# Where the token numbers of a routed mixture-of-experts kernel are multiplied in

## The chip, the core and the metric

The kernel runs on one core of a Trainium2 chip. The metric is the device time of one execution, in microseconds. It is compared as the median of several executions of the same program.

## The reference

Three layers follow each other: a chunked attention, a soft mixture of experts, and a top-2 routed mixture of experts. The change touches the third alone, which is given here without its first lines (three matrix products and a log1p that yield `noisy_logits`, 3072 x 8):

```python
N, D, E, F = 3072, 512, 8, 1024
top2 = np.argpartition(-noisy_logits, 2, axis=1)[:, :2]
top2_l = np.take_along_axis(noisy_logits, top2, axis=1)
top2_l = top2_l - top2_l.max(-1, keepdims=True)
top2_w = np.exp(top2_l)
top2_w /= top2_w.sum(-1, keepdims=True) + 1e-09
out = np.zeros((N, D), dtype=np.float32)
for e in range(E):
    for k in range(2):
        mask = top2[:, k] == e
        if not mask.any():
            continue
        h = np.maximum(x[mask] @ w1[e], 0.0)
        out[mask] += top2_w[mask, k, None] * (h @ w2[e])
```

So each of 3072 tokens has two experts, and 6144 token-expert pairs go through a 512-1024-512 network of their expert.

## The kernel before, in words

`experts` sorts the 6144 pairs into 48 tiles of 128 slots, with experts in an order of ranks 0 to 7 that depends on the data. Rank 0 fills the first six tiles by construction, ranks 1 to 7 the rest. A few more tiles stand behind a branch and are not used with this input. Instructions are issued in the order of the source, so each engine runs its own instructions in the order in which `experts` calls the helpers.

**A tile in the loop** (index `n`, tile `i`): `gather(i)` fetches 128 rows of a table by token number (POOL, an indirect DMA through `idx`). `ct(i)` transposes them on PE, with a copy on ACT. `l1(i)` is eight matmuls with the rank's first matrix `G`, then a relu into `hi` on ACT, and `lo(i)` puts the rest that float16 loses into `lo` on DVE. `l2(i)` is 24 matmuls: eight of `hi` with the float16 second matrix, eight of `hi` with that matrix's low part, and eight of `lo` with the float16 second matrix. `yv(i)` scales on ACT, and `put(i)` adds the rows into two output tensors by two indirect DMAs on POOL. In the loop, step `n` issues gather(n+6), ct(n+2), l1(n+1) and l2(n), in this order on PE: ct, l1, l2. Tiles 0 to 5 use `G` in place; from tile 6 on `gcopy` (SP) copies the rank's `G` into the buffer `C` or `CT`, and the first layer of tile 6 waits for that.

**Preparing a rank's weights** (`prep_*`, rank `rk`): a product of all slot outputs with the first matrix (`prep_g`, PE), maxima of both matrices (`prep_gmax`, `prep_max`, DVE; `bound`, ACT), two transposes on PE that spread the maxima over the partitions (`prep_row`, `prep_all`) with a reduction on DVE between them, scale factors (`prep_s`, `prep_inv`), the scaled `G` (`prep_gs`, ACT and DVE), and the second matrix in four parts, each as a float16 high part (`prep_hi`, ACT) and a low part (`prep_lo`, DVE, L428). `plan(n, ...)` puts such a step into loop step `n` ahead of `l2`; `mid(n, ...)` puts it inside `l2`, ahead of its last eight matmuls.

**Finding the token of each slot.** `bases` and `positions` (DVE) give each pair its slot, split into a column `ns` within a tile and a tile number `tq`. `spread_s` makes 48 one-hot matrices of 128 x 128 from `ns` (L544 on DVE, L537 and L540 on ACT), `tiles` (L812) compares `tq` with the tile numbers, and POOL multiplies the result by the token numbers `K["val"]` (L813). `inverse` sums 48 products of the two on PE (L647), and `finish_idx` (DVE, L655 to L658) turns that into `idx` for tiles 6 and up, which the gathers of tiles 6 and later need. `tile_tables` (L780 to L797) gives each tile its rank (`rti`). `wide_w` (POOL) makes the gate weights that go into the table. All of this stands between the first tiles of rank 0, which have an index of their own.

Of the kernel before, what the change touches and what calls it, by code (L numbers as in the profile page):

```python
# [14 lines left out]
OP = mybir.AluOpType  # L15
# [10 lines left out]
NT = N // 128  # L26
# [9 lines left out]
NSL = NTL + 2  # L36
# [2 lines left out]

RB = 12  # L40
NA0, NP0 = 7, 5
NA2, NP2 = 16, 0
ORDER = [('qk', 29), ('mx', 29), ('s0', 29), ('tr', 31), ('sub', 29), ('exp', 29), ('s1', 29), ('av', 27), ('nrm', 27), ('lt', 5), ('ltc', 5), ('qk', 30), ('max', 0), ('at', 28), ('atc', 28), ('mx', 30), ('qk', 31), ('col', 0), ('at', 29), ('s0', 30), ('sub', 30), ('atc', 29), ('pc', 15), ('exp', 30), ('colc', 0), ('av', 28), ('bc', 0), ('nrm', 28), ('pc', 14), ('xt', 26), ('dsub', 0), ('mx', 31), ('xtc', 26), ('s1', 30), ('ex', 0), ('sub', 31), ('ldv', 31), ('exp', 31), ('at', 30), ('s0', 31), ('atc', 30), ('av', 29), ('xt', 28), ('xt', 27), ('mm', 0, 0, 0), ('nrm', 29), ('s1', 31), ('at', 31), ('atc', 31), ('xtc', 27), ('xtc', 28), ('av', 30), ('nrm', 30), ('xt', 29), ('av', 31), ('xt', 30), ('mm', 0, 0, 1), ('xtc', 29), ('xtc', 30), ('lg', 6), ('nrm', 31), ('mm', 0, 1, 1), ('xt', 31), ('lgc', 6), ('xtc', 31), ('es', 0), ('lg', 7), ('lt', 6), ('lgc', 7), ('lt', 7), ('ltc', 6), ('esp', 0), ('mm', 0, 2, 1), ('ltc', 7), ('mm', 0, 3, 1), ('mm', 0, 1, 0), ('max', 1), ('col', 1), ('mm', 0, 2, 0), ('colc', 1), ('bc', 1), ('dsub', 1), ('fac',), ('mm', 0, 3, 0), ('ex', 1), ('mm', 1, 0, 0), ('facx',), ('out', 0, 0), ('out', 0, 1), ('es', 1), ('mm', 1, 1, 0), ('esp', 1), ('out', 1, 0), ('w',), ('mm', 1, 0, 1), ('mm', 1, 1, 1), ('sit', 0), ('out', 1, 1), ('sitc', 0), ('sit', 1), ('sitc', 1)]
CF = {}
C16 = {}
# [261 lines left out]
def experts(tc, nc, C, CT, SOT, sog, wgn, nz, zt, table, mw1, mw2, out, K, K16, rw, rt, ew, ps):  # L307
# [119 lines left out]
        w2, hi, lo = w2p(rk, part)  # L427
        stt(lo, w2, sc[:, rk, 5:6], hi, op0=OP.mult, op1=OP.subtract)  # L428

    def prep_lop(rk, part):  # L430
        w2, hi, lo = w2p(rk, part)
        t = W2r[:, 7 * 4096 + 3072:8 * 4096]
        nc.gpsimd.tensor_tensor(t, w2, bc(sc[:, rk, 5:6], 1024), OP.mult)
        nc.gpsimd.tensor_tensor(lo, t, hi, OP.subtract)

    s4 = T(5)

    def bound(x, vec=False, half=None):
# [365 lines left out]
        vt(t, s4[:, 2:4], AX.X, OP.max)  # L804
        tt(sc[:, rk, 1:2], sc[:, rk, 1:2], t, OP.max)

    J2 = cut(48, NA2, NP2)
    o2 = oh_t[:, :, T0:NSL]

    def tiles(k):  # L810
        o, q = [x[:, NT * k:NT * k + NT] for x in (o2, tq)]
        tt(o, bc(K16["t128"][:, None, T0:NSL], NT, NSL - T0), bc(q[:, :, None], NT, NSL - T0), OP.is_equal)  # L812
        nc.gpsimd.tensor_tensor(o, o, bc(K["val"][:, :, None], NT, NSL - T0), OP.mult)  # L813

    finish_idx(0, T0)
    gather(0)
# [13 lines left out]
        gather(i)  # L830
    ct(0)
    prep_hi(0, 2)
    bases()
    ns, tq = positions()
    gcopy(0)
    gcopy(1)
    gcopy(2)
# [5 lines left out]
    gates2()  # L843
    prep_inv(0)
    ts(gw0, gw0, sc[:, 0, 6:7], 2.0 ** -10, op0=OP.mult, op1=OP.mult)
    prep_lop(0, 3)
    wide_w()
    tiles(0)
    prep_lo(0, 0)
    tiles(1)  # L850
    l2(0, (0,), 2)
    l1(1, False)
    l2(0, (1,), 2)
    lo(1)
    prep_lo(0, 1)
    prep_lo(0, 2)
    load_e(1, 1)
    nc.sync.dma_start(table[0:N, 64:ROW].rearrange("(t p) c -> p t c", p=128), wd)
    spread_s(oh_s, ns, J2[0], J2[1], J2[2][:16])
    l2(1, (0, 1), 2)  # L860
    prep_g(1)
    ct(2)
    l2(0, (2,), 2)
    l1(2)
    gate(0)
    yv(0)
    spread_s(oh_s, ns, [], [], J2[2][16:])
    prep_max(1, 0, 2)
    bound(2)
    ct(3)  # L870
    bound(3)
    join_max(1)
    put(0)
    PLAN, MID = {}, {}

    def plan(i, f, *a):
# [29 lines left out]
    for n, i in enumerate(seq):
# [460 lines left out]
```

## Time and profile before

| | |
|---|---|
| median of 3 runs | 600.06 us (598.2 to 609.83) |
| profiled execution: its own time, its span | 601.2 us, 599.4 us |
| busy in the span: PE, DVE, ACT, POOL | 498.9, 332.0, 291.6, 290.3 us |
| mean granted clock of TensorE | 0.936 |

The first 230 us are attention and the soft layer, which the change leaves alone. The routed layer prepares itself until about 304 us and then runs tile after tile. A busy share is an average over these stages, so it does not say which engine ends a given stage. That is read from the waits in the stage, and from the chain of work that ended last. A duration in the timeline is that of an instruction from its start to its end, and successive instructions of one engine overlap a little; where a sequence is priced, the distance between starts is used.

### The profile page before, as it was taken

How to read it: one execution, taken by the hardware profiler on the slowest of the kernel's cores; microseconds unless marked ns; L12 is line 12 of the kernel's file. 1: busy time of each engine (PE TensorE's matmuls, PEld its weight loads, DVE VectorE, ACT ScalarE, POOL GpSimd, SP SyncE). 2: the span in 40 equal slices, each digit the busy share in tenths (PEclk: the TensorE clock that was granted, in tenths of full speed). 3: DMA queues.
4: the chain of work that ended last, by engine and by line, in shares of the span. 5: the costliest groups of instructions: out<-in, count | busy, mean ns of one | idle time of the engine just before them, and what ended most of it. 6: DMA issues, size and time to landing. Idle time of an engine off the chain costs nothing.

```text
span 599.4 us, 15297 instructions
## 1 busy us (share of the span) xinstructions
PE 498.9 (83%) x5437; PEld 274.1 (46%) x5437; DVE 332.0 (55%) x827; ACT 291.6 (49%) x510; POOL 290.3 (48%) x260
## 2 busy tenths in 40 slices
PE   5776988869889677365989899999999999989960
PEld 4655766647543124232534445545545455435520
DVE  6565767657863004898565755748566465622200
ACT  5876989868521104753532715526354263533210
POOL 6132322222012000693566765758576577877662
PEclk9998999999999867597989989999999999989995
DMA  9999999999999998959388696887869876436552
GB/s 206 231 217 213 241 240 262 229 221 241 315 412 362 412 415 241 349 179 254 52 248 226 111 265 152 233 226 170 224 150 264 215 183 119 80 69 111 75 63 26
DMA packets 99509, 127.35 MB, mean 212 GB/s; under 512 B 19238, under 2 KB 68026, under 8 KB 99434
## 3 DMA queue, kind: packets, MB, share of 16 engines
q1 hardware_dynamic: 79866, 109.30, 60.7%
q0 software_dynamic: 19152, 16.89, 21.2%
q8 instruction: 49, 0.80, 0.6%
q14 instruction: 26, 0.21, 0.1%
q10 hardware_dynamic: 416, 0.15, 0.1%
HBM read 94.84 MB, written 20.42 MB: 192 GB/s over the span
## 4 chain that ended last, share of the span: by engine, by line
PE 37%; DVE 7%; DMA 5%; issue 4%; POOL 3%; ACT 2%; SPq 0%; POOLq 0%; DVEq 0%; ACTq 0%
PE l L739 30%; DMA out_dram<-y,idx 4%; PE l L705 3%; POOL out_dram L770 2%; PE g L362 2%; DVE W L428 1%; DMA C<-G 1%; DVE W L544 1%; PE l L736 1%; DVE lo L715 1%; POOL cg L664 1%; ACT W L424 1%; DVE G L411 1%; DVE W L812 1%; ACT hi L707 0%
## 5 line engine op out<-in xcount | busy, mean ns | idle before, releaser
L770 POOL DMA_INDIRECT out_dram<-y,idx x96 | 155.8, 1622 | 83.3 <-DMA out_dram<-y,idx 40.7
L739 PE MATMUL l<-W,hi 128*128 (+1 forms) x768 | 182.5, 392 | 1.2 <-DVE W L428 0.8
L715 DVE SCALAR_TENSOR_TENSOR lo<-l,hi 128x1024 f16<-128x1024 f32 x49 | 59.9, 1222 | 112.3 <-ACT hi L707 97.8
L739 PEld LDWEIGHTS <-hi 128*128 128x128 f16 x768 | 75.2, 100 | 88.9 <-issue 14.3
L757 ACT ACTIVATE y<-l,gw 128x512 f32<-128x512 f32 x49 | 33.5, 684 | 156.1 <-PE l L739 94.0
L739 PE MATMUL l<-W,lo 128*128 (+1 forms) x384 | 90.8, 379 | 4.6 <-DVE lo L715 4.6
L1022 POOL DMA_DIRECT2D arena<-in_mem_v_dram x64 | 39.3, 615 | 105.1 <-PE av L1112 105.1
L664 POOL DMA_INDIRECT cg<-table,idx x49 | 51.1, 1044 | 20.4 <-issue 10.5
L739 PEld LDWEIGHTS <-lo 128*128 128x128 f16 x384 | 36.9, 98 | 48.5 <-DVE lo L715 5.2
L707 ACT ACTIVATE hi<-l 128x1024 f16<-128x1024 f32 x49 | 50.2, 1024 | 10.3 <-PE l L705 10.2
L1069 PE MATMUL st<-arena,qT 128*32 128x112 f32 (+2 forms) x768 | 31.8, 271 | 16.2 <-ACT arena L1050 9.9
L428 DVE SCALAR_TENSOR_TENSOR W<-w,sc,W 128x1024 f16<-128x1024 f32 x31 | 42.3, 1390 | 0.2
L1050 ACT ACTIVATE qT<-tr 64x384 f32<-64x384 f32 x64 | 33.2, 518 | 9.3 <-PE tr L1043 8.2
L1033 DVE COPY arena<-arena 32x768 f32<-32x768 f32 x32 | 17.8, 556 | 35.2 <-DMA arena<-in_v_dram 30.6
L1043 PE MATMUL tr<-cf,arena 128*128 128x128 f32 x192 | 31.2, 304 | 6.2 <-DMA arena<-in_q_dram 5.4
L424 ACT ACTIVATE W<-w,sc 128x1024 f16<-128x1024 f32 x32 | 35.7, 1149 | 0.2
L1112 PE MATMUL av<-arena,aT 128*32 128x130 f32 x768 | 29.3, 283 | 4.2 <-issue 3.5
L1050 ACT ACTIVATE arena<-tr 64x384 f32<-64x384 f32 x64 | 30.9, 484 | 2.3 <-PE tr L1043 1.6
L374 DVE TENSOR_REDUCE mxp<-w 128x1 f32<-128x2048 f32 x13 | 29.6, 2275 | 0.0
L1043 PEld LDWEIGHTS tr<-cf,arena 128*128 128x128 f32 x192 | 22.9, 153 | 13.8 <-issue 6.7
L1062 PE MATMUL st<-arena,qT 128*32 128x16 f32 x768 | 25.7, 188 | 2.8 <-issue 2.8
L1031 ACT ACTIVATE arena<-arena 32x768 f32<-32x768 f32 x32 | 26.9, 842 | 1.6 <-issue 0.7
(268 smaller groups left out, 680.3 us busy)
## 6 DMA issues: line engine op xcount, KB each, us to landing
w<-in_moe_w_dram SPq DMA_DIRECT2D x88, 512.0 KB
arena<-in_moe_w_dram SPq DMA_DIRECT2D x28, 512.0 KB
arena<-in_v_dram SPq DMA_DIRECT2D x62, 168.0 KB
arena<-in_q_dram SPq DMA_DIRECT2D x16, 384.0 KB
arena<-in_k_dram SPq DMA_DIRECT2D x16, 384.0 KB
xs<-in_moe_w_dram SPq DMA_DIRECT2D x12, 512.0 KB
out_dram<-zt SPq DMA_DIRECT2D x14, 384.0 KB
C<-G SPq DMA_DIRECT2D x21, 256.0 KB
```

What stands on the lines that cost most here:

```text
L424: nc.scalar.activation(hi, w2, AF.Copy, scale=sc[:, rk, 5:6])
L428: stt(lo, w2, sc[:, rk, 5:6], hi, op0=OP.mult, op1=OP.subtract)
L664: nc.gpsimd.indirect_dma_start(out=CG[i], out_offset=None, in_=table, in_offset=bass.IndirectOffsetOnAxis(ap=idx[:, i:i + 1], axis=0))
L707: nc.scalar.activation(HI[i], p, AF.Relu)
L715: stt(LO[i].rearrange("p k t -> p (k t)"), p.rearrange("p k t -> p (k t)"), 0.0, HI[i].rearrange("p k t -> p (k t)"), op0=OP.max, op1=OP.s ...
L739: nc.tensor.matmul(P2[i], h[i][:, k, :], dyn(W2f, i, w * 4096 + 512 * k, 512, RG.get(i)), start=x == 0 and k == 0, stop=x == last and k == 7)
L757: nc.scalar.activation(YV[i], P2.pop(i), AF.Copy, scale=GW.pop(i))
L770: nc.gpsimd.indirect_dma_start(out=o, out_offset=bass.IndirectOffsetOnAxis(ap=idx[:, i:i + 1], axis=0), in_=y[:, DH * h:DH * h + DH], in_o ...
L1022: nc.gpsimd.dma_start(vcols(i, p + 28, 4, col, 128), bass.AP(tensor=mem_v.tensor, offset=mem_v.offset + (b * H + 2 * hp + h) * NMEM * D, a ...
L1043: nc.tensor.transpose(p[:, T, :], src[:, h, T, :], identf)
L1050: nc.scalar.activation(o, i, AF.Copy)
L1069: nc.tensor.matmul(st[32 * j:32 * j + 32, g, :, w0:w1], QT[u][:, 32 * c:32 * c + 32], kb[:, :, 16 * c + w0:16 * c + w1], start=True, stop= ...
```

## The change

DVE makes all 48 one-hot matrices, with the token number multiplied in by the same instruction (`spread_v`, one `tensor_scalar` with two operations and two columns of scalars). The products by POOL in `tiles`, and the 16 one-hots of ACT, are gone. `prep_lop`, which made one low part of rank 0 on POOL, is gone too, and DVE makes all four, two of them ahead of `lo(0)`. `bases`, `positions` and `wide_w` come after the low parts, `tiles` and the one-hots after the first layer of tile 2. For rank 1, `prep_row` moves from step 2 to step 3, `prep_all` from inside step 2's `l2` to step 4, and the steps that follow one step later. `inverse` and the gathers of tiles 6 to 9 move from step 2 to step 3, behind `tile_tables`.

```diff
@@ experts
-    def prep_lop(rk, part):
-        w2, hi, lo = w2p(rk, part)
-        t = W2r[:, 7 * 4096 + 3072:8 * 4096]
-        nc.gpsimd.tensor_tensor(t, w2, bc(sc[:, rk, 5:6], 1024), OP.mult)
-        nc.gpsimd.tensor_tensor(lo, t, hi, OP.subtract)
...
     def tiles(k):
         o, q = [x[:, NT * k:NT * k + NT] for x in (o2, tq)]
         tt(o, bc(K16["t128"][:, None, T0:NSL], NT, NSL - T0), bc(q[:, :, None], NT, NSL - T0), OP.is_equal)
-        nc.gpsimd.tensor_tensor(o, o, bc(K["val"][:, :, None], NT, NSL - T0), OP.mult)
+
+    def spread_v(js):
+        for j in js:
+            ts(oh_s[:, j, :], K16["ni128"], ns[:, j:j + 1], K["val"][:, j % NT:j % NT + 1], op0=OP.is_equal, op1=OP.mult)
...
     ct(0)
     prep_hi(0, 2)
-    bases()
-    ns, tq = positions()
+    prep_lo(0, 0)
+    prep_lo(0, 1)
     gcopy(0)
...
-    prep_lop(0, 3)
-    wide_w()
-    tiles(0)
-    prep_lo(0, 0)
-    tiles(1)
     l2(0, (0,), 2)
     l1(1, False)
     l2(0, (1,), 2)
+    prep_lo(0, 2)
     lo(1)
-    prep_lo(0, 1)
-    prep_lo(0, 2)
+    prep_lo(0, 3)
     load_e(1, 1)
+    bases()
+    ns, tq = positions()
+    wide_w()
     nc.sync.dma_start(table[0:N, 64:ROW].rearrange("(t p) c -> p t c", p=128), wd)
-    spread_s(oh_s, ns, J2[0], J2[1], J2[2][:16])
-    l2(1, (0, 1), 2)
-    prep_g(1)
-    ct(2)
     l2(0, (2,), 2)
-    l1(2)
     gate(0)
     yv(0)
-    spread_s(oh_s, ns, [], [], J2[2][16:])
+    put(0)
+    ct(2)
+    l2(1, (0, 1), 2)
+    l1(2)
+    tiles(0)
+    tiles(1)
+    prep_g(1)
+    spread_v(range(24))
+    ct(3)
+    spread_v(range(24, 48))
     prep_max(1, 0, 2)
     bound(2)
-    ct(3)
     bound(3)
     join_max(1)
-    put(0)
...
         if rk == 1:
-            plan(a + 2, prep_row, rk)
-            mid(a + 2, prep_all, rk)
-            late = (3, 3, 4, 4, 4)
+            mid(a + 3, prep_row, rk)
+            plan(a + 4, prep_all, rk)
+            late = (4, 4, 5, 5, 5)
...
-        if n == 2:
-            inverse(oh_s, o2, [*J2[2], *J2[1], *J2[0]], T0, NSL)
+        if n == 3:
+            inverse(oh_s, o2, range(48), T0, NSL)
...
-        if n > 2:
+        elif n > 1:
             put(i)
```

The order of the instructions shows two places. The first is DVE from the end of the ordering of the ranks on: `W2<-w` is a low part of the second matrix, `lo` the rest of a relu, and `W2<-c16` a comparison of `tiles` (24x56) or a one-hot (128x128). Before:

```order
L599 CAST eid_3286<-W2_3293 128x8
...
L530 TENSOR_SCALAR W2_3293<-W2_3293 128x48
L715 SCALAR_TENSOR_TENSOR lo_3632<-l1_3591,hi_3600 128x1024
...
L812 TENSOR_TENSOR W2_3293<-c16_2871,W2_3293 128x24x56
L428 SCALAR_TENSOR_TENSOR W2_3293<-w_3240,sc_3292,W2_3293 128x1024
L812 TENSOR_TENSOR W2_3293<-c16_2871,W2_3293 128x24x56
L715 SCALAR_TENSOR_TENSOR lo_3676<-l1_3657,hi_3666 128x1024
L428 SCALAR_TENSOR_TENSOR W2_3293<-w_3240,sc_3292,W2_3293 128x1024 x2
L544 TENSOR_SCALAR W2_3293<-c16_2871,W2_3293 128x128 x16
```

and now:

```order
L592 CAST eid_3286<-W2_3293 128x8
L427 SCALAR_TENSOR_TENSOR W2_3293<-w_3240,sc_3292,W2_3293 128x1024 x2
L708 SCALAR_TENSOR_TENSOR lo_3620<-l1_3579,hi_3588 128x1024
...
L427 SCALAR_TENSOR_TENSOR W2_3293<-w_3240,sc_3292,W2_3293 128x1024
L708 SCALAR_TENSOR_TENSOR lo_3655<-l1_3635,hi_3644 128x1024
L427 SCALAR_TENSOR_TENSOR W2_3293<-w_3240,sc_3292,W2_3293 128x1024
...
L523 TENSOR_SCALAR W2_3293<-W2_3293 128x48
L708 SCALAR_TENSOR_TENSOR lo_3724<-l1_3713,hi_3722 128x1024
L804 TENSOR_TENSOR W2_3293<-c16_2871,W2_3293 128x24x56 x2
L367 TENSOR_REDUCE sc_3292<-g_3728 128x1
L808 TENSOR_SCALAR W2_3293<-c16_2871,W2_3293,cfb_2874 128x128 x48
```

The four low parts now stand ahead of the slot positions (which end at L530, now L523), and the third relu rest (`lo_3724`, tile 2) stands ahead of the comparisons and of one row of 48 one-hots.

The second place is PE around the inverse (`ct<-W2`, 48 matmuls); `ct<-c16,cg` is a tile's transpose, and of a run of equal rows the first stands here. Before:

```order
L739 MATMUL l2_3846<-W2_3293,lo_3776 128x512
...
L647 MATMUL ct_3874<-W2_3293 128x56
...
L669 MATMUL ct_3938<-c16_2871,cg_3570 128x128
...
L705 MATMUL l1_3942<-ctt_3826,G_3294 128x128
...
L739 MATMUL l2_3988<-W2_3293,hi_3837 128x512
...
L739 MATMUL l2_3988<-W2_3293,lo_3839 128x512
...
L669 MATMUL ct_4019<-c16_2871,cg_3928 128x128
```

and now:

```order
L381 MATMUL g_3728<-cf_60,sc_3292 2x128
...
L732 MATMUL l2_3899<-W2_3293,lo_3835 128x512
...
L640 MATMUL ct_3929<-W2_3293 128x56
...
L662 MATMUL ct_3995<-c16_2871,cg_3983 128x128
...
L698 MATMUL l1_3999<-ctt_3870,G_3294 128x128
...
L387 MATMUL g_3728<-cf_60,mxr_3917 128x2
...
L732 MATMUL l2_4043<-W2_3293,hi_3881 128x512
```

Before, the transpose behind the inverse is that of tile 5 (`cg_3570`), and the second layer of tile 3 (24 matmuls, `l2_3988`) stands between the inverse and the transpose of tile 6 (`cg_3928`). Now the transpose of tile 6 (`cg_3983`), whose gather needs the inverse, stands directly behind it, and the first layer of tile 5 and rank 1's second transpose (L387) stand behind that.

## Rows read from the trace of the kernel before

**Rows 1.** Busy time by stretch: stretch, its length, each engine, granted clock, DMA.

```profile
260.00:270.00 10.00, 6.31 (x54) 2.70 (x53) 10.00 (x6) 5.44 (x14) 9.92 (x4) 1.00 0.28 85
...
400.00:530.00 130.00, 129.31 (x902) 64.74 (x900) 76.73 (x161) 59.51 (x95) 89.98 (x64) 1.00 0.72 174
```

**Rows 2.** Chain of work that ended last: start, length, engine, work.

```profile
265.68 5.63 DVE W L428 x2
...
288.21 1.25 PE ct L647 x48
...
301.24 2.45 DMA C<-G
303.73 0.62 PE l L705 x8
```

**Rows 3.** DVE in time, 250 to 281 us: start, length, line, operation.

```profile
250.81 0.21 DVE L606 TENSOR_TENSOR W<-W 128x64 f32<-128x64 f32 x1
...
254.51 2.62 DVE L529 SCALAR_TENSOR_TENSOR W<-W 128x48 f32<-128x48 f32 x1
...
257.15 1.21 DVE L715 SCALAR_TENSOR_TENSOR lo<-l,hi 128x1024 f16<-128x1024 f32 x1
...
259.68 1.54 DVE L812 TENSOR_TENSOR W<-c,W 128x1344 f16<-128x1344 f16 x1
...
271.23 2.68 DVE L544 TENSOR_SCALAR W<-c,W 128x128 f16<-128x128 f16 x16
...
275.30 2.97 DVE L544 TENSOR_SCALAR W<-c,W 128x128 f16<-128x128 f16 x16
...
280.64 0.16 DVE L805 TENSOR_TENSOR sc<-sc,mxp 128x1 f32<-128x1 f32 x1
```

**Rows 4.** POOL in time: start, length, line, operation, and the idle time before.

```profile
245.72 1.08 POOL L664 DMA_INDIRECT cg<-table,idx  x1 [2.25 <-ACT G L410]
...
263.09 7.13 POOL L813 TENSOR_TENSOR W<-W,cfb 128x1344 f16<-128x1344 f16 x2
...
290.87 1.01 POOL L664 DMA_INDIRECT cg<-table,idx  x1 [3.99 <-DVE idx L658]
...
529.85 1.01 POOL L664 DMA_INDIRECT cg<-table,idx  x1 [0.30 <-PE l L739]
```

**Rows 5.** ACT in time, 252 to 264 us.

```profile
252.42 1.02 ACT L707 ACTIVATE hi<-l 128x1024 f16<-128x1024 f32 x1
...
257.57 1.02 ACT L707 ACTIVATE hi<-l 128x1024 f16<-128x1024 f32 x1 [2.92 <-PE l L705]
258.49 4.77 ACT L537 ACTIVATE W<-c,W 128x128 f16<-128x128 f16 x16
```

**Rows 6.** DVE in time, 289 to 307 us.

```profile
289.74 0.19 DVE L655 TENSOR_SCALAR W<-W 128x56 f32<-128x56 f32 x1 [7.62 <-ACT W L940]
289.85 0.24 DVE L656 TENSOR_SCALAR W<-W,cfb 128x56 f32<-128x56 f32 x1
...
292.66 0.21 DVE L394 TENSOR_SCALAR sc<-g 128x1 f32<-128x1 f32 x2
...
296.83 0.42 DVE L413 COPY G<-G 32x1024 f16<-32x1024 f16 x1
...
298.49 0.16 DVE L780 TENSOR_TENSOR W<-W 128x8 f32<-128x8 f32 x1
...
303.29 3.67 DVE L428 SCALAR_TENSOR_TENSOR W<-w,sc,W 128x1024 f16<-128x1024 f32 x3
```

**Rows 7.** PE in time: start, length, line, operation, and the idle time before.

```profile
250.67 0.29 PE L669 MATMUL ct<-c,cg 128*128 128x128 f16 x1 [6.72 <-DMA cg<-table,idx]
...
281.02 5.21 PE L739 MATMUL l<-W,hi 128*128 128x512 f16 x16
...
290.26 3.62 PE L739 MATMUL l<-W,hi 128*128 128x512 f16 x16
...
532.24 0.23 PE L669 MATMUL ct<-c,cg 128*128 128x128 f16 x1 [2.48 <-DMA cg<-table,idx]
```

More of the change, by code (lines that the diff above doesn't have):

```diff
@@ L41 @@
 NA0, NP0 = 7, 5
-NA2, NP2 = 16, 0
 ORDER = [('qk', 29), ('mx', 29), ('s0', 29), ('tr', 31), ('sub', 29), ('exp', 29), ('s1', 29), ('av', 27), ('nrm', 27), ('lt', 5), ('ltc', 5), ('qk', 30), ('max', 0), ('at', 28), ('atc', 28), ('mx', 30), ('qk', 31), ('col', 0), ('at', 29), ('s0', 30), ('sub', 30), ('atc', 29), ('pc', 15), ('exp', 30), ('colc', 0), ('av', 28), ('bc', 0), ('nrm', 28), ('pc', 14), ('xt', 26), ('dsub', 0), ('mx', 31), ('xtc', 26), ('s1', 30), ('ex', 0), ('sub', 31), ('ldv', 31), ('exp', 31), ('at', 30), ('s0', 31), ('atc', 30), ('av', 29), ('xt', 28), ('xt', 27), ('mm', 0, 0, 0), ('nrm', 29), ('s1', 31), ('at', 31), ('atc', 31), ('xtc', 27), ('xtc', 28), ('av', 30), ('nrm', 30), ('xt', 29), ('av', 31), ('xt', 30), ('mm', 0, 0, 1), ('xtc', 29), ('xtc', 30), ('lg', 6), ('nrm', 31), ('mm', 0, 1, 1), ('xt', 31), ('lgc', 6), ('xtc', 31), ('es', 0), ('lg', 7), ('lt', 6), ('lgc', 7), ('lt', 7), ('ltc', 6), ('esp', 0), ('mm', 0, 2, 1), ('ltc', 7), ('mm', 0, 3, 1), ('mm', 0, 1, 0), ('max', 1), ('col', 1), ('mm', 0, 2, 0), ('colc', 1), ('bc', 1), ('dsub', 1), ('fac',), ('mm', 0, 3, 0), ('ex', 1), ('mm', 1, 0, 0), ('facx',), ('out', 0, 0), ('out', 0, 1), ('es', 1), ('mm', 1, 1, 0), ('esp', 1), ('out', 1, 0), ('w',), ('mm', 1, 0, 1), ('mm', 1, 1, 1), ('sit', 0), ('out', 1, 1), ('sitc', 0), ('sit', 1), ('sitc', 1)]
@@ L805, in join_max @@
         tt(sc[:, rk, 1:2], sc[:, rk, 1:2], t, OP.max)
-    J2 = cut(48, NA2, NP2)
     o2 = oh_t[:, :, T0:NSL]
```

## The prediction

> **What bounds the kernel now.** I read the busy time by stretch first. Between 400 and 530 us PE is busy for 129.3 of 130 us at full clock [rows 1]: there the tiles follow each other with no gap, and nothing but the number of matmuls sets the pace. The change removes no matmul. So it can only shift the moment at which this run of tiles starts. The chain of waits names that moment: the first layer of tile 6 starts at 303.73 us, behind a copy of rank 1's first matrix that the chain gives as 2.45 us from 301.24 us [rows 2]. Up to there the chain runs over DVE in the 260s and 270s, then over PE with the inverse (48 matmuls at 288.21 us). From 260 to 270 us DVE is busy for all 10.00 us and POOL for 9.92, PE for 6.31 [rows 1]. The timeline tells why DVE is so full there: two low parts take 5.63 us beside POOL's products with the token numbers (7.13 us from 263.09 us) [rows 2, 4], where three of the same kind take 3.67 us later [rows 6]. That is 2.8 us each against 1.2. So the stretch before 304 us is what to price, and its end, the first layer of tile 6, is what to compare. After that the same work follows in the same order, so I carry any shift there to the end of the run unchanged; POOL's output writes close it, and those of each tile wait for that tile's second layer.
>
> **The change, step by step.** I lay the new order out with starts in us of the span; where two engines meet, the later one counts.
>
> 1. *Low parts first.* DVE is free at 250.81 [rows 3]. Two low parts at 1.2 [rows 6] end at 253.3. The relu of tile 0 ends on ACT at 253.44 [rows 5], its rest (1.15) at 254.6; the four small gate instructions (from 258.36 to 259.68 in the old order [rows 3], 1.3) end at 255.9, the third low part at 257.1. The relu of tile 1 ends at 258.59 [rows 5], unchanged, since what PE does until then is unchanged; its rest ends at 259.7, the fourth low part at 260.9. The gate weights on POOL run beside this and may cost DVE a few tenths, which the wait for the relu absorbs.
>
> 2. *Slot positions.* From 250.81 to 254.51 the old order spends 3.7 on them, then 2.62 on one instruction of 48 columns [rows 3], where one of 56 columns costs 0.2 [rows 6]. That long one stood beside POOL's low part, which is gone. I take 0.2, and 0.1 for the last one: positions ready at 264.9. If the 2.62 comes back, the slack of step 3 takes 1.6 of it.
>
> 3. *Tiles 0 to 2 on PE.* With the fourth low part ready, tile 0 is done at 261.4. Sixteen matmuls of tile 1 take 3.5 at full clock [rows 7], the first layer of tile 2 0.6 [rows 2]: 265.5. Relu 1.0 and rest 1.2: DVE goes on at 267.7, having idled from 264.9 to 266.5. ACT no longer makes 16 one-hots (4.77 [rows 5]); nothing on the path waited for ACT there, so I cost that at nothing.
>
> 4. *Comparisons and one-hots on DVE.* Two comparisons at 1.5 [rows 3], uncontended: 270.7. The maximum behind them 0.2 (from 273.91, the end of the first sixteen one-hots, to 275.30, less a relu rest): 270.9. Then 48 one-hots. No row has this instruction with two columns of scalars. With one column sixteen take 2.68 or, beside POOL's output writes, 2.97 [rows 3]: 0.168 and 0.186 each. Below stands 0.168, since a second operation is no reason for a gain; above, the extra 0.05 that L656 (two operations, one column) shows over L655 (one operation, none) [rows 6]: 0.24. I take 0.18, nearest to the rows of the same shape: 8.6 us, until 279.5.
>
>    The Trainium skill, VectorE: DVE Perf Modes, section on the 4x mode, says that in this mode the second operation runs in slices that every element passes through anyway, so it would cost nothing. By that the 48 would take 8.1 us instead of 8.6. No run here shows it yet.
>
> 5. *Maximum, rests, tile tables.* Maximum and join 2.5 (from 278.27 to 280.80 [rows 3]): 282.0. The rest of tile 3 until 283.2, of tile 4 until 284.4. The tile tables, now ahead of the index, 3.6 (from 298.49 to 303.29 less a rest of 1.2 [rows 6]): 288.0. One small reduction: 288.2.
>
> 6. *PE meanwhile.* Tile 2 needs nothing that is late and ends near 275.5, tile 3's first sixteen matmuls near 279.3. Its last eight wait for the rest at 283.2. After such a wait of some 3.4 us the old trace shows sixteen matmuls at 5.21 instead of 3.62 [rows 7], so about eight at half clock; I take 3.4 for these eight: 286.6. Inverse 1.3 [rows 2]: 287.9; the copy behind it 0.3 (up to 289.74 [rows 6]): 288.2, level with DVE.
>
> 7. *Index, gather, transpose.* From the first index instruction to the gather 1.1 (289.74 to 290.87 [rows 6, 4]): 289.3. The gather holds POOL for 1.0: 290.3. Landing: in the tail a transpose that waited for its gather started 1.4 after POOL was done (530.86 to 532.24); the first gather took 3.9 (246.80 to 250.67), beside the zeroing of the output [rows 4, 7]. At 290 us nothing large is in flight, since rank 2's first matrix is loaded long before, so I take 1.4: 291.7. **This wait is new:** in the old order the second layer of tile 3 stood between, and now the first layer of tile 5 and rank 1's second transpose are queued behind it on PE.
>
> 8. *Rank 1's matrix.* Transpose 0.2, first layer of tile 5 at half clock 1.0: 292.9. Relu 1.0, rest 1.2: 295.1. From the first factor to the finished matrix 4.6 (292.66 to 297.25 [rows 6]): 299.7. SyncE's issue 0.2 and copy 2.5 [rows 2]: **302.4**, against 303.73.
>
> The second layer of tile 4 ends near 299, so PE waits for the copy, as before, and the matmuls behind it start at the lower clock, as before. Rank 1's other low parts end near 309, the second layer of tile 6 starts near 312: hidden. The loads of rank 2's second matrix, queued on SyncE behind these parts, leave about 2 us later than before and are needed near 313: hidden.
>
> So what was saved early (tile 0 is finished 11 us sooner) is nearly all given back, because the index of tile 6 hangs on DVE and everything else on that index. **The sum is -1.3 us**, against the profiled execution of 601.2 us (span 599.4): 599.9. The median shown is 1.1 lower, 600.06, so the median to expect is 598.8, say 599.
>
> **The rivals.**
>
> *A. Dear one-hots: slower.* At a price p the 48 move the start by 48 x (p - 0.18). From p = 0.21 on the gain of 1.3 is gone. At 0.24 the median becomes 601.7 (+1.6); at 0.30, 604.6. For it: no row has two columns of scalars, and L656 is slower than L655. Against: the difference there is 0.05. Chance 17%.
>
> *B. A late gather: slower.* If tile 6's gather takes 3.9 to land, the start moves by 2.5, to a median of 601.3. For it: both indirect writes of tile 2 are near it in POOL's queue. Against: the row of the tail, with writes around it as well. Chance 13%.
>
> *C. The preparation gets out of the way.* If the new chain is shorter by 3 or 4 us than I have it (one-hots at 0.168, full clock at steps 6 and 8, tile tables at 3.0 without POOL beside them), the copy arrives about when PE ends tile 4, and PE's own work becomes the limit: first layer of tile 6 at 298.5 to 300, -4 to -5, a median of 595 to 596. For it: each of my prices in steps 5, 6 and 8 was taken beside other engines. Against: it needs all of them. Chance 18%.
>
> *D. The change does not reach the start at all*, because something after it sets the pace, such as POOL's writes: no change, 600.1. Against: PE's 129.3 of 130 us. Chance 4%.
>
> **How the numbers follow.** My own case, -2.8 to +0.5 around the sum's 598.8, has 48%. C reaches down to 595.5, A and B up to 603; beyond lie a one-hot price over 0.28 and whatever I have not seen. The range 595.5 to 603 leaves out some 2 in 10, and the three runs shown, 598.2 to 609.83, say that it can't be narrower. About 2%, or 12 us, is what a measurement of this kernel can tell from no change. Only a one-hot of more than 0.45 us, or an unseen stall, is slower than that; faster by that much isn't in the profile, since PE's work behind tile 6 stays. So: faster 3%, within 94%, slower 3%.
>
> **What the profile afterwards would show.** Right: POOL without a long product between 255 and 275 us; low parts at 1.2 each; tile 0's output written near 263; 48 one-hots in one block of about 8.6 us that ends near 279.5; two waits on PE, for the rest of tile 3 and, ahead of tile 6's transpose, for its gather; the first layer of tile 6 behind the copy near 302.4. Wrong: one-hots over 0.2 each (step 4), an index much earlier than 289 (steps 5 and 6), the copy not awaited by PE (step 8). The forecast itself is wrong if the first layer of tile 6 moves by more than 4 us either way, or if the run of tiles behind it has gaps that it did not have.

## The result, and the profile of the changed kernel

The changed kernel's median is 604.34 us (19 runs), that of the kernel before 602.55 (19 runs, taken beside them). The ratio is 1.0059, 95% interval 1.0030 to 1.0087: slower by 0.3 to 0.9%, which is under the 2% that I had called the limit of no change, but on the other side from my -1.3 us, and 604.34 lies above my range. A second measurement of both on another chip gave 0.9999 (0.9959 to 1.0040). So the change buys nothing, and costs up to some 5 us. Medians are over all executions, while the ratios leave out those more than 1.5% above the fastest of their kernel, so a ratio is not always the quotient of the two medians.

The profiled execution of the changed kernel spans 609.3 us. It reaches the routed layer 7 us later than the one of before, because stages that the change doesn't touch took longer in that execution. I therefore count from a common point: **the mark** is the time from DVE's cast of the expert numbers (tile `eid`) to the first layer of tile 6. The cast starts at 250.51 us in the kernel before, the first layer at 303.73 [rows 2]: 53.22 us. My forecast of 302.4 was a mark of 51.9.

DVE of the changed kernel in time (start and length in us, engine, line, operation, tiles, count, idle time before with what ended it):

```profile
257.51 0.38 DVE L592 CAST eid<-W 128x8 int32<-128x8 f32 x1
261.24 1.23 DVE L708 SCALAR_TENSOR_TENSOR lo<-l,hi 128x1024 f16<-128x1024 f32 x1 [0.71 <-ACT hi L700]
266.81 1.23 DVE L708 SCALAR_TENSOR_TENSOR lo<-l,hi 128x1024 f16<-128x1024 f32 x1 [1.08 <-ACT hi L700]
...
274.98 1.23 DVE L708 SCALAR_TENSOR_TENSOR lo<-l,hi 128x1024 f16<-128x1024 f32 x1 [1.80 <-ACT hi L700]
276.12 3.02 DVE L804 TENSOR_TENSOR W<-c,W 128x1344 f16<-128x1344 f16 x2
...
279.39 10.79 DVE L808 TENSOR_SCALAR W<-c,W,cfb 128x128 f16<-128x128 f16 x48
290.10 2.27 DVE L373 TENSOR_REDUCE mxp<-w 128x1 f32<-128x2048 f32 x1
...
292.66 0.16 DVE L798 TENSOR_TENSOR sc<-sc,mxp 128x1 f32<-128x1 f32 x1
292.74 2.35 DVE L708 SCALAR_TENSOR_TENSOR lo<-l,hi 128x1024 f16<-128x1024 f32 x2
295.00 0.16 DVE L773 TENSOR_TENSOR W<-W 128x8 f32<-128x8 f32 x1
...
298.94 0.17 DVE L648 TENSOR_SCALAR W<-W 128x56 f32<-128x56 f32 x1
```

L808 is the block of one-hots: 48 in 10.79 us, 0.225 us each, where 16 with one column took 2.68 or 2.97 before [rows 3]. Behind it stand the maximum and its join (290.10 to 292.7), two rests, the tile tables from 295.00 and the index from 298.94, each as soon as the one ahead of it is done. Nothing on DVE waits in between, so whatever the one-hots cost should arrive at the index in full; experiment 8 tests that.

PE of the changed kernel in the same stretch, same columns:

```profile
283.60 3.62 PE L732 MATMUL l<-W,hi 128*128 128x512 f16 x16
292.88 0.37 PE L381 MATMUL g<-cf,sc 128*2 128x128 f32 x1 [5.66 <-DVE sc L798]
294.01 3.25 PE L732 MATMUL l<-W,lo 128*128 128x512 f16 x8 [0.77 <-DVE lo L708]
297.10 1.40 PE L640 MATMUL ct<-W 128*128 128x56 f16 x48
302.55 0.23 PE L662 MATMUL ct<-c,cg 128*128 128x128 f16 x1 [4.05 <-DMA cg<-table,idx]
302.62 0.61 PE L698 MATMUL l<-ctt,G 128*128 128x128 f16 x8
...
312.55 0.62 PE L698 MATMUL l<-ctt,C 128*128 128x128 f16 x8 [2.15 <-DMA C<-G]
```

Up to the transpose of tile 6, PE stands still three times: 5.66 us for the maximum (a transpose of rank 1's preparation asks for it), 0.77 for the rest of tile 3, and 4.05 for the gather of tile 6. A fourth wait, 2.15 us for the copy of rank 1's matrix, ends at the mark. The inverse (L640) is over at 298.5, and yet the transpose behind it starts at 302.55, because the index on DVE (from 298.94), the gather on POOL (until 301.05) and its landing stand between. The mark is 312.55 - 257.51 = 55.04 us.

POOL issues that gather in the row below. Busy time by stretch follows it, with the columns of [rows 1] (stretch, length, busy time and instructions of PE, PEld, DVE, ACT and POOL, granted clock, DMA share, GB/s):

```profile
300.04 1.01 POOL L657 DMA_INDIRECT cg<-table,idx  x1 [1.51 <-DVE idx L651]
```

```profile
280.00:290.00 10.00, 7.22 (x41) 3.33 (x38) 10.00 (x46) 1.86 (x4) 5.53 (x4) 1.00 0.65 129
290.00:300.00 10.00, 4.86 (x57) 2.50 (x57) 9.28 (x25) 0.91 (x2) 0.95 (x1) 0.66 0.01 1
...
400.00:530.00 130.00, 129.40 (x903) 64.73 (x902) 77.37 (x166) 59.84 (x97) 88.58 (x62) 1.00 0.77 184
```

From 280 to 300 us DVE is busy for 19.28 of 20 us and PE for 12.08: DVE bounds this stretch. From 400 to 530 us PE has hardly a gap, as before.

### The profile page after: what moved, and what is told of

Same layout as the page of the kernel before. It is cut to its first block, busy times and chain, and to the rows that moved or that the text cites. A ratio compares the mean times of both kernels' runs of the same rounds, so it can differ in the third digit from the quotient of the medians.

```text
span 609.3 us, 15292 instructions
## 1 busy us (share of the span) xinstructions
PE 498.7 (82%) x5437; PEld 276.2 (45%) x5437; DVE 332.1 (55%) x844; ACT 285.1 (47%) x493; POOL 277.9 (46%) x256
## 5 line engine op out<-in xcount | busy, mean ns | idle before, releaser
L732 PE MATMUL l<-W,hi 128*128 (+1 forms) x768 | 180.1, 389 | 0.7 <-ACT hi L700 0.4
L732 PE MATMUL l<-W,lo 128*128 (+1 forms) x384 | 92.4, 384 | 0.8 <-DVE lo L708 0.8
L657 POOL DMA_INDIRECT cg<-table,idx x49 | 52.8, 1077 | 17.9 <-issue 11.9
L700 ACT ACTIVATE hi<-l 128x1024 f16<-128x1024 f32 x49 | 50.2, 1024 | 10.8 <-PE l L698 7.1
L427 DVE SCALAR_TENSOR_TENSOR W<-w,sc,W 128x1024 f16<-128x1024 f32 x32 | 40.4, 1287 | 0.2
L1087 ACT ACTIVATE a<-a 128x384 f32<-128x384 f32 x32 | 16.8, 524 | 25.3 <-DVE a L1083 24.8
```

Of the source, the lines that this page charges most:

```text
L657: nc.gpsimd.indirect_dma_start(out=CG[i], out_offset=None, in_=table, in_offset=bass.IndirectOffsetOnAxis(ap=idx[:, i:i + 1], axis=0))
L700: nc.scalar.activation(HI[i], p, AF.Relu)
L732: nc.tensor.matmul(P2[i], h[i][:, k, :], dyn(W2f, i, w * 4096 + 512 * k, 512, RG.get(i)), start=x == 0 and k == 0, stop=x == last and k == 7)
```

## The experiments

All marks are counted as above, and each is from one trace.

**1. The changed kernel again.**

> The changed kernel once more, beside the kernel before on the same chip. The marker of all runs is the time from the start of the cast of the expert order (eid, DVE) to the start of the first layer of tile 6 (first matmul that reads C): 303.73 - 250.51 = 53.2 us before, 312.55 - 257.51 = 55.0 us in the first trace of the change. Theory 1 (the stretch itself is longer, by dear one-hots and new waits on DVE): the marker is 55 again within 1 us, and the 48 one-hots take 10.5 to 11 us again. Theory 2 (the first trace was a disturbed execution, the stretch isn't longer): marker 52 to 53.5, one-hots near 8.6 us.

Measured: mark 55.25 us, ratio 0.9999 (0.9959 to 1.0040), 12 runs. The one-hots again took 10.79 us:

```profile
252.00 0.38 DVE L592 CAST eid<-W 128x8 int32<-128x8 f32 x1
273.22 10.79 DVE L808 TENSOR_SCALAR W<-c,W,cfb 128x128 f16<-128x128 f16 x48
283.93 2.28 DVE L373 TENSOR_REDUCE mxp<-w 128x1 f32<-128x2048 f32 x1
293.06 0.19 DVE L648 TENSOR_SCALAR W<-W 128x56 f32<-128x56 f32 x1 [0.23 <-ACT W L935]
```

The mark repeats to 0.2 us here, and the 7 us by which the first trace came later are not the change's: here the cast is at 252.00. The index waits 0.23 us for ACT's copy of the inverse, so PE's way to the index, through the maximum, the rest of tile 3 and the inverse, is level with DVE's.

**2. The kernel before again.**

> The kernel before, unchanged, for a second trace. If the mark is a property of the program: 53.2 within 0.3 us. If it wanders from one execution to the next: off by 1 us or more, and differences of the mark below that say nothing.

Measured: cast at 253.78, first layer of tile 6 at 308.21, a mark of 54.43, 1.21 us over that of the first trace. So the second answer holds: the mark of the kernel before wanders by some 1.2 us. Nearly all of it lies in one row of PE, sixteen matmuls that take 6.22 us here and 5.21 in the first trace [rows 7], behind a wait of the same length:

```profile
284.33 0.37 PE L382 MATMUL g<-cf,sc 128*2 128x128 f32 x1 [3.71 <-DVE sc L805]
284.50 6.22 PE L739 MATMUL l<-W,hi 128*128 128x512 f16 x16
```

In the first trace the granted clock is 0.50, the lower of its two levels, from 281 to 284 us and 1.00 from 285 on. Here it is 0.50 from 285 to 288 and still 0.71 from 288 to 291, so the lower level lasts longer. From here on I read differences of the mark under 1.2 us as nothing. The change costs 0.6 to 2.0 us at the mark, which fits both ratios.

A part of this wander evens out right behind the mark. The sixteen matmuls of tile 6, in the first trace of the kernel before and, below it, in this one:

```profile
304.19 5.30 PE L739 MATMUL l<-W,hi 128*128 128x512 f16 x16
```

```profile
308.67 3.62 PE L739 MATMUL l<-W,hi 128*128 128x512 f16 x16
```

What this trace lost ahead of the mark, the first one loses behind it. The first layer of tile 7 starts 60.60 and 60.12 us after the cast in the kernel before, and 62.42 and 62.63 in the changed kernel. There the change costs 1.8 to 2.5 us, with a wander of 0.5 and 0.2.

**3. The inverse behind tile 2 again**, with the index and the gathers of tiles 6 to 9:

```diff
-        if n == 3:
+        if n == 2:
             inverse(oh_s, o2, range(48), T0, NSL)
...
-        elif n > 1:
+        if n > 2:
             put(i)
```

> The inverse, the index of tiles 6 on and their gathers back at loop step 2, all else as changed. Theory 1 (the index of tile 6 is late because its four DVE instructions stand behind the tile tables and behind the rest of tile 4, and PE waits for it twice): the index is ready some 4 to 5 us earlier, the wait ahead of tile 6's transpose goes, DVE's idle 4.5 us ahead of the rest of tile 5 go; marker 50 to 51, about 4 us under the changed kernel and 2 under before. Theory 2 (only the one-hots' price counts, where the inverse stands is neutral): marker 55 within 1 us.

Measured: mark 51.96, ratio to the kernel before 0.9911 (0.9857 to 0.9966). The medians say less: 604.24 us (12 runs), 605.34 (12) for the changed kernel and 604.96 (29) for the kernel before, all on the same occasion. PE, at the inverse and at the mark:

```profile
283.78 7.37 PE L640 MATMUL ct<-W 128*128 128x56 f16 x48
291.45 0.27 PE L662 MATMUL ct<-c,cg 128*128 128x128 f16 x1 [0.31 <-ACT W L935]
...
311.27 1.03 PE L698 MATMUL l<-ctt,C 128*128 128x128 f16 x8 [5.42 <-DMA C<-G]
```

The 48 matmuls of the inverse now stretch over 7.37 us, since they follow DVE's one-hots one by one. That looks worse than 1.40 us, but the second layer of tile 3 then runs under the gather, and no wait for the gather is left. What ends the stretch is the copy of rank 1's matrix, 5.42 us. So the inverse's move costs the changed kernel 3.1 to 3.3 us at the mark, and 2.0 to 2.2 at the first layer of tile 7 (60.44). For the whole time the ratio says as much and the medians do not, so that stays open.

**4. The inverse a tile later, alone, in the kernel before.**

```diff
-        if n == 2:
+        if n == 3:
             inverse(oh_s, o2, [*J2[2], *J2[1], *J2[0]], T0, NSL)
...
-        if n > 2:
+        elif n > 1:
             put(i)
```

> The kernel before with one part of the change alone: the inverse, the index and the gathers of tiles 6 to 9 behind tile 3 and not behind tile 2. Mark as before (from DVE's cast of the expert numbers to the first layer of tile 6; 53.2 in the kernel before). Theory (the inverse a tile later costs by itself: tile 6's transpose then waits on PE for its gather, and the second layer of tile 4 stands behind it): mark 55.2 to 57.2, a wait of 3 us or more for the gather ahead of tile 6's transpose. Rival (DVE's wait of 7.6 us for the inverse goes, rank 1's matrix is made earlier and makes up for it): mark 52 to 53.5.

Measured: cast at 249.50, first layer of tile 6 at 313.93, a mark of 64.43; ratio 1.0080 (1.0022 to 1.0137). The theory's side, with 10 to 11 us where it said 2 to 4. PE, and below it the first instruction of the index on DVE:

```profile
294.85 1.40 PE L647 MATMUL ct<-W 128*128 128x56 f16 x48
306.03 0.29 PE L669 MATMUL ct<-c,cg 128*128 128x128 f16 x1 [9.78 <-DMA cg<-table,idx]
306.97 5.35 PE L739 MATMUL l<-W,hi 128*128 128x512 f16 x16
```

```profile
301.72 0.18 DVE L655 TENSOR_SCALAR W<-W 128x56 f32<-128x56 f32 x1
```

The inverse ends at 296.25, but the index is made from 301.72 on: the kernel before has the tile tables on DVE ahead of it in that place, from 298.07 until then. I had forgotten in my expectation what I had put into step 5 of the prediction. A wait of 9.78 us follows, and the sixteen matmuls behind it take 5.35 us (granted clock 0.50 from 307 to 309 us), where 3.62 is their time at full clock. Of the 10 to 11 us at the mark, 7 to 9 are left between the cast and the end of the span (355.9 us against 348.9 and 346.8).

**5. The slot positions ahead of the first expert's low parts again.**

```diff
+    bases()
+    ns, tq = positions()
     prep_lo(0, 0)
     prep_lo(0, 1)
...
-    bases()
-    ns, tq = positions()
     wide_w()
```

> The slot positions back ahead of the low parts of rank 0, as before the change; all else as changed. Theory 1 (the low parts depend on the first gathers by way of the relus, so DVE waits 0.7, 0.9, 1.1 and 1.8 us, which the positions used to fill): the one-hots start 2 to 2.5 us earlier after the cast, marker 52.5 to 53.3. Theory 2 (those waits are slack, since tile 0 must be finished first for the rest of tile 2): the one-hots start within 0.7 us of the changed kernel, marker 54.3 to 55.7.

Measured: mark 58.23, ratio 1.0091 (1.0050 to 1.0132). Both stated theories are wrong: 3.0 to 3.2 us slower, where I had a gain or nothing. DVE shows why:

```profile
260.61 1.21 DVE L708 SCALAR_TENSOR_TENSOR lo<-l,hi 128x1024 f16<-128x1024 f32 x1
...
271.96 1.23 DVE L708 SCALAR_TENSOR_TENSOR lo<-l,hi 128x1024 f16<-128x1024 f32 x1 [5.97 <-ACT hi L700]
273.11 3.02 DVE L804 TENSOR_TENSOR W<-c,W 128x1344 f16<-128x1344 f16 x2
```

and PE, in the second layer of tile 0:

```profile
261.87 3.26 PE L732 MATMUL l<-W,lo 128*128 128x512 f16 x8 [1.87 <-DVE lo L708]
```

The positions are early, and nobody can use them: the comparisons stand behind the rest of tile 2, which waits 5.97 us for tile 2's relu, and so for PE. PE in turn waited 1.87 us for the rest of tile 0, which DVE reaches behind the positions and two low parts. The one-hots start 23.9 us after the cast, not 21.2 to 21.9. By the mark and the ratio "low parts first" is thus a gain of the change, and in this order the start of the comparisons is set by PE's first layer of tile 2.

**6. The price of a one-hot.** Three blocks of 16 one-hots, with nothing else added, stand ahead of the routed layer's first instructions, where POOL has no work on data: one operation with one column of scalars, two operations with a column and a constant, two operations with two columns.

```diff
+    for j in range(16):
+        ts(oh_s[:, j, :], K16["ni128"], K["val"][:, j:j + 1], None, op0=OP.is_equal)
+    for j in range(16):
+        ts(oh_s[:, 16 + j, :], K16["ni128"], K["val"][:, j:j + 1], 1.0, op0=OP.is_equal, op1=OP.mult)
+    for j in range(16):
+        ts(oh_s[:, 32 + j, :], K16["ni128"], K["val"][:, j:j + 1], K["val"][:, j:j + 1], op0=OP.is_equal, op1=OP.mult)
```

> The changed kernel with three times 16 extra one-hot instructions of 128x128 at the start of the routed layer, where POOL issues nothing and the results are overwritten later: one operation with a scalar column; two operations, the second with a constant; two operations with two scalar columns. Only their own durations are read; the run as a whole gets some 10 us longer. Theory 1 (the second column is what costs): 0.165, 0.165 and 0.225 us each. Rival a (the second operation costs): 0.165, 0.225 and 0.225. Rival b (neither; the changed kernel's one-hots are slowed by POOL's output writes beside them): all three 0.165 to 0.175.

Measured (one run, 614.73 us with the 9 us that the blocks add):

```profile
232.40 2.69 DVE L352 TENSOR_SCALAR W<-c,cfb 128x128 f16<-128x128 f16 x16 [0.31 <-DMA w<-in_moe_w_dram]
235.01 2.68 DVE L354 TENSOR_SCALAR W<-c,cfb 128x128 f16<-128x128 f16 x16
237.61 3.65 DVE L356 TENSOR_SCALAR W<-c,cfb 128x128 f16<-128x128 f16 x16
```

Start to start, the first two blocks take 2.61 and 2.60 us, 0.163 each; the third takes 3.65 until its end, about 0.225 each. A second operation with a constant costs nothing, the second column of scalars costs 0.06 us, and with POOL quiet the price is that of the changed kernel. The Trainium skill, VectorE: DVE Perf Modes, section on the 4x mode, puts the first and the second operation into different slices of the same pass, which gives four results per cycle with both; by that a second operation takes no time of its own, and the first two rows agree.

**7. The product with the token numbers on POOL again**, in the changed kernel's order.

```diff
         tt(o, bc(K16["t128"][:, None, T0:NSL], NT, NSL - T0), bc(q[:, :, None], NT, NSL - T0), OP.is_equal)
+        nc.gpsimd.tensor_tensor(o, o, bc(K["val"][:, :, None], NT, NSL - T0), OP.mult)
...
-            ts(oh_s[:, j, :], K16["ni128"], ns[:, j:j + 1], K["val"][:, j % NT:j % NT + 1], op0=OP.is_equal, op1=OP.mult)
+            ts(oh_s[:, j, :], K16["ni128"], ns[:, j:j + 1], None, op0=OP.is_equal)
```

> The order of the changed kernel, but the product with the token numbers goes back to POOL (two instructions of some 7 us behind the comparisons) and the 48 one-hots of DVE have one column of scalars again. Mark: from DVE's cast of the expert numbers to the first layer of tile 6, 55.04 and 55.25 us in the two traces of the changed kernel. Theory (the second column is what the mis-sized term is made of, 48 x 0.06 us, and DVE's chain sets the mark): one-hots at 0.163 to 0.186 each, mark 52.3 to 53.4. Rival (POOL's products slow DVE beside them, as they slowed the low parts from 1.2 to 2.8 us): one-hots over 0.20 each, mark 54.5 or more.

Measured: mark 55.80, ratio 0.9958 (0.9895 to 1.0022), so no gain at the mark. The rival holds. POOL's row, and below it the one-hots on DVE, read once up to POOL's end and once after it:

```profile
271.40 6.08 POOL L805 TENSOR_TENSOR W<-W,cfb 128x1344 f16<-128x1344 f16 x2 [3.34 <-DVE W L804]
```

```profile
273.03 4.50 DVE L809 TENSOR_SCALAR W<-c,W 128x128 f16<-128x128 f16 x2
```

```profile
277.45 7.80 DVE L809 TENSOR_SCALAR W<-c,W 128x128 f16<-128x128 f16 x46
```

While POOL's two products run (until 275.08 and 277.49), two one-hots take 4.50 us and end at 275.13 and 277.53, each within 0.05 us of a product's end; the other 46 take 7.80, 0.17 each. The block is not slower throughout, it nearly stands still and then runs at its price. So the second column cost 2.1 us against my forecast, and not against the alternative: with the product on POOL the 48 take 12.2 us, and with the second column 10.8. The Trainium skill, SBUF — State Buffer, section on the two sides of SBUF, says that GpSimd and a DVE instruction in a mode with two ports exclude each other for the whole instruction; these rows agree.

**8. The maximum on ACT**, so that the reduction and the join leave DVE's chain.

```diff
-    prep_max(1, 0, 2)
-    bound(2)
-    bound(3)
-    join_max(1)
+    for x in range(4):
+        bound(x)
+    vt(sc[:, 1, 1:2], s4[:, :4], AX.X, OP.max)
```

> The changed kernel, but the maximum of rank 1's second matrix is taken wholly by ACT (four bounds instead of two, and one small maximum on DVE), which takes the reduction and the join, some 2.4 us, off DVE between the one-hots and the tile tables. Theory (DVE's chain from the comparisons to the index sets the start of tile 6): the mark falls from 55.1 by 2.0 to 2.4, to 52.7 to 53.2; time 0.4% under the changed kernel's. Rival (DVE's chain has slack, and PE's second layers and the rests they wait for set it): mark 54.5 to 55.5, no change.

Measured: cast at 252.92, first layer of tile 6 at 305.05, mark 52.13, 2.9 to 3.1 under the changed kernel; median 600.58 (6 runs) against 606.23 (20 runs) for the kernel before, without an interval. The theory holds: what leaves DVE between the one-hots and the index, some 2.4 us, arrives at the mark in full (the 0.5 to 0.7 beyond it is within what the mark wanders). The wait for the gather is still there (3.88 us), since the whole chain moved with it:

```profile
294.48 0.29 PE L662 MATMUL ct<-c,cg 128*128 128x128 f16 x1 [3.88 <-DMA cg<-table,idx]
...
305.05 0.62 PE L698 MATMUL l<-ctt,C 128*128 128x128 f16 x8 [1.47 <-DMA C<-G]
```

**9. The rest of tile 2 behind the first 24 one-hots.**

```diff
-    l1(2)
+    l1(2, False)
     tiles(0)
     tiles(1)
-    prep_g(1)
     spread_v(range(24))
+    lo(2)
+    prep_g(1)
```

> The changed kernel, but the rest of tile 2 is issued to DVE behind both comparisons and the first 24 one-hots, not ahead of the comparisons, so that DVE doesn't wait for tile 2's relu (it waited 1.8 us there). Theory (the wait for PE's first layer of tile 2 sits on the chain that ends in the index): the mark falls from 55.1 by 1.5 to 2.0. Rival (the second layer of tile 2, which now starts later, holds PE up, and the inverse with it): mark 55 or more.

A small maximum on DVE (from `prep_g`) moves behind the 24 one-hots with it. Measured: cast at 253.12, first layer of tile 6 at 307.15, mark 54.03, 1.0 to 1.2 under the changed kernel; ratio 0.9989 (0.9915 to 1.0064). The one-hots began 18.7 us after the cast, not 21.2 to 21.9. This lies between the two expectations and within what the mark wanders: inconclusive by itself.

**10. Rank 1's transposes a tile earlier again**, the inverse left behind tile 3.

```diff
-            mid(a + 3, prep_row, rk)
-            plan(a + 4, prep_all, rk)
-            late = (4, 4, 5, 5, 5)
+            plan(a + 2, prep_row, rk)
+            mid(a + 2, prep_all, rk)
+            late = (3, 3, 4, 4, 4)
```

> The changed kernel with rank 1's transposes, factors and low parts one tile earlier again, as in the kernel before; the inverse stays behind tile 3. Theory (this part of the change was needed: the maximum is ready only behind the 48 one-hots, and a transpose that asks for it a tile earlier holds up the second layer of tile 2 on PE): mark 58 to 61, over the 55.1 of the changed kernel. Rival (the later transposes are what delays rank 1's matrix): mark 52 to 54.

Measured (one run, 618.67 us): cast at 254.69, first layer of tile 6 at 319.93, mark 65.24, some 10 over the changed kernel. The theory's side, and larger than it said:

```profile
288.86 0.37 PE L381 MATMUL g<-cf,sc 128*2 128x128 f32 x1 [14.79 <-DVE sc L798]
...
312.82 0.29 PE L662 MATMUL ct<-c,cg 128*128 128x128 f16 x1 [9.92 <-DMA cg<-table,idx]
```

PE waits 14.79 us for a maximum that DVE reaches behind the 48 one-hots, with the second layer of tile 2 behind it in its queue. With the one-hots in one block on DVE, the transposes had to move.

**11. and 12. What the runs point to, together**: the inverse behind tile 2, the maximum on ACT, the rest of tile 2 behind 24 one-hots (as in 3, 8 and 9), and rank 1's transposes and factors around the second layer of tile 3:

```diff
-            mid(a + 3, prep_row, rk)
-            plan(a + 4, prep_all, rk)
+            plan(a + 3, prep_row, rk)
+            for f in (prep_all, prep_s, prep_inv, prep_gs):
+                mid(a + 3, f, rk)
             late = (4, 4, 5, 5, 5)
...
-        plan(a + late[0], prep_s, rk)
-        plan(a + late[0], prep_inv, rk)
-        plan(a + late[0], prep_gs, rk)
+        if rk > 1:
+            for f in (prep_s, prep_inv, prep_gs):
+                plan(a + late[0], f, rk)
```

> All that the runs point to at once, on the changed kernel: the inverse, the index and the gathers of tiles 6 to 9 behind tile 2 again, the maximum on ACT, the rest of tile 2 behind 24 one-hots, and rank 1's rows and factors as soon as tile 4 is reached. Theory (DVE's chain sets the start, and what is taken off it comes through until PE's own work ahead of tile 6 is the limit): mark 46 to 48.5 us, 7 us under the changed kernel's, ratio to the kernel before about 0.985 to 0.99. Rival (the last copy of rank 1's matrix waits for the relu and the rest of tile 5 at half clock whatever comes ahead of it): mark 50 to 52, as with the inverse alone.

> The best version once more, on another occasion, for its time and a second trace. If the first measurement (0.9795, interval 0.972 to 0.987) was right: ratio 0.975 to 0.99, mark 46.4 to 47.1 us. If it was luck of that occasion: ratio above 0.99.

Measured: 599.22 us against 606.23, ratio 0.9795 (0.9720 to 0.9870, 6 runs); on the second occasion 596.82 against 604.67, ratio 0.9870 (0.9827 to 0.9913, 12 runs). Marks 46.74 and 45.55. By the medians this version is 1.2 and 1.3% under the kernel before. It was not measured beside the changed kernel, which was not faster than the kernel before on either occasion. PE of its first trace:

```profile
277.98 1.90 PE L732 MATMUL l<-W,lo 128*128 128x512 f16 x8 [1.26 <-DVE lo L708]
279.72 4.15 PE L640 MATMUL ct<-W 128*128 128x56 f16 x48
284.18 0.22 PE L662 MATMUL ct<-c,cg 128*128 128x128 f16 x1 [0.31 <-ACT W L936]
...
300.40 0.62 PE L698 MATMUL l<-ctt,C 128*128 128x128 f16 x8 [2.61 <-DMA C<-G]
```

None of the three waits of the changed kernel is left; PE waits for the rest of tile 2 and, at the end, for the copy.

**How far the shifts last.** The same traces tell when later tiles start. Start of the first layer in us after the cast:

| trace | tile 6 (mark) | tile 7 | tile 20 |
|---|---|---|---|
| kernel before, and again | 53.2, 54.4 | 60.6, 60.1 | 145.6, 145.0 |
| changed kernel, and again | 55.0, 55.3 | 62.4, 62.6 | 146.2, 148.4 |
| 3, inverse behind tile 2 | 52.0 | 60.4 | 146.2 |
| 4, inverse later in the kernel before | 64.4 | 70.1 | 155.9 |
| 5, positions first | 58.2 | 63.9 | 148.9 |
| 7, product on POOL | 55.8 | 63.2 | 149.2 |
| 8, maximum on ACT | 52.1 | 57.8 | 142.4 |
| 9, rest of tile 2 later | 54.0 | 59.7 | 145.4 |
| 10, transposes earlier | 65.2 | 70.9 | 155.4 |
| 11 and 12, together | 46.7, 45.6 | 54.1, 51.6 | 137.5, 136.9 |

Up to tile 20 two traces of the changed kernel come to differ by 2.2 us. The shifts of 4, 8, 10, 11 and 12 are larger and last; those of 3, 5, 7 and 9 can't be told from this wander there. Experiment 6 is left out, since its blocks delay the cast against the first gathers.

## Why the prediction was wrong, step by step

The forecast was -1.3 us against the trace of before; the two traces of the changed kernel show +1.8 and +2.0 at the mark against that trace, and +0.6 and +0.8 against the second one of before. From the cast to the end of the span they take 351.8 us both, those of before 348.9 and 346.8, so the loss does not all lie ahead of the mark, where the forecast had put the whole shift; a wait near the end, told in the last section, is about 2 us longer. Set against the starts of my steps, in us after the cast:

| start of | predicted | changed kernel | again |
|---|---|---|---|
| rest of tile 0 (step 1) | 2.9 | 3.7 | 3.1 |
| rest of tile 1 (step 1) | 8.1 | 9.3 | 8.6 |
| rest of tile 2 (step 3) | 16.0 | 17.5 | 16.8 |
| one-hots (step 4) | 20.4 | 21.9 | 21.2 |
| maximum, behind the one-hots (step 5) | 29.0 | 32.6 | 31.9 |
| index (step 7) | 37.7 | 41.4 | 41.1 |
| transpose of tile 6 (step 7) | 41.2 | 45.0 | 44.7 |
| first layer of tile 6 (step 8) | 51.9 | 55.0 | 55.3 |

- **Step 4 is the step that failed**: 0.225 us per one-hot and not 0.18, so the term is 10.8 and not 8.6 us, 2.1 of the 3.1 to 3.4 us that the mark was missed by. The mechanism that the forecast named, an index that hangs on DVE's chain, is right; this term was mis-sized. Experiment 6 shows that it is the second column. I had the bound (0.24) and chose the low end by the shape of the rows, and looked at the number of operations, which costs nothing, rather than at that of the columns.
- **Steps 1 and 3** were 0.8 to 1.5 us short at the start of the one-hots. The most part is there already at the rest of tile 1, which waited for its relu (0.71 and 1.08 us ahead of the rests of tiles 0 and 1). I had held that relu's time "unchanged"; it came 0.5 and 1.2 us later. The traces show two causes. The transpose of tile 0 starts 0.93 us after the cast in the first trace, held up by its gather, 0.27 in the second and 0.16 in the trace of before. And the first layer of tile 1 takes 1.06 us in both, at a granted clock of 0.50, where it took 0.64 before. The second trace of the kernel before has 1.06 as well, and its relu of tile 1 ends 8.6 us after the cast, as in the second of the changed kernel. So 0.5 us of this is a wander that the kernel before shows as well; the rest, in the first trace alone, is the late gather, and why it was late is open. The rows of the first trace:

```profile
258.44 0.29 PE L662 MATMUL ct<-c,cg 128*128 128x128 f16 x1 [7.49 <-DMA cg<-table,idx]
...
264.65 1.06 PE L698 MATMUL l<-ctt,G 128*128 128x128 f16 x8
```

- **Step 2** held: the positions run without the long instruction of before, and wait for tile 2 afterwards (1.80 us; I had 1.6).
- **Step 5** held: 8.8 and 9.2 us from the end of the one-hots to the index, 8.7 predicted.
- **Step 6** held: the eight matmuls behind the wait took 3.25 and 3.59 us (3.4 predicted). The wait itself, 3.9 predicted and all of it for the rest of tile 3, was 5.66 for the maximum and 0.77 for the rest, longer mainly by what step 4 missed.
- **Step 7** held, with its new wait: 4.05 and 3.93 us for the gather (3.8 predicted), which landed 1.5 us after POOL was done (1.4 predicted). I had seen the wait and let the tile tables stand ahead of the index as given; experiment 3 shows that putting the inverse back is worth 3.1 to 3.3 us at the mark, which would then lie under that of the kernel before (51.96 against 53.22 and 54.43). The wait stood in the sum, so it is what the change costs, and not why the forecast missed.
- **Step 8** held: 9.9 and 10.5 us from the first layer of tile 5 to that of tile 6, 10.5 predicted.

**Rival A** is what happened, at a price between the 0.21 from which the gain is gone and its 0.24: 0.225 makes 48 x 0.045 = 2.2 us, or +0.9 us against the trace of before; steps 1 and 3 make the rest. (By its formula the range's upper end, 603, answers to a price of 0.27, not 0.28.) **Rival B** is refuted by the landing of 1.5 us. **Rival C** did not come about by the change, but the version of experiment 11 shows that the room was there: 45.6 to 46.7 us at the mark. **Rival D** is refuted: experiments 4, 8 and 11 move the mark by 3 to 11 us, the shift is still there at tile 20, and the time goes the same way.

The level was off too. I carried my difference to 600.06 us, a median of three; 19 and more runs of the same kernel gave 602.55, 604.96, 606.23 and 604.67. About 2.5 of the 5.3 us by which 599.0 misses 604.34 are the level's, the rest the change's.

## What to carry to other kernels

Price an instruction from a row that has the same kinds of operands, its columns of scalars above all; where there is none, take the dear bound on a chain that has no slack. When a step moves later, ask what its engine's queue holds ahead of its result: here the index stood behind one-hots, a maximum, two rests and the tile tables, and moving the producer a tile later moved the matmuls that used to hide the gather in front of it. A producer that runs slowly, one piece at a time behind its source, can still be better than one that runs fast and late.

## What was not expected of the hardware

- A one-hot of 128 x 128 in f16 with two columns of scalars takes 0.225 us, with one column 0.163, and a second operation with a constant adds nothing.
- Beside two products of POOL that took 6.08 us, two of DVE's one-hots took 4.50 us, and the 46 after them 7.80.
- One wait comes and goes between executions: in the last part of the run a transpose waits for a gather for 2.48 and 2.43 us in the two traces of the kernel before, 4.94 and 4.20 in those of the changed kernel. In the version of experiment 11 it waits 4.19 us, in the second trace of the same program not at all. The row is that of the first trace:

```profile
529.21 0.23 PE L662 MATMUL ct<-c,cg 128*128 128x128 f16 x1 [4.19 <-DMA cg<-table,idx]
```

  What decides it stays open. It makes single executions of one kernel differ by up to some 4 us, and is why the mark, and not the span, was compared.
